# Linear attention and a gated FFN in one kernel: a new order of the first batch's loads and turns, the second batch's turns all by DMA, later loads for batches three and four

## The chip, the cores and the metric

The kernel runs on one core of one Trainium2 chip. The metric is the time of one execution on the device in microseconds (us). Before the change the median of 12 runs is 573.68 us (572.44 to 574.38). Engines are named as in the profile: PE (TensorE), DVE (VectorE), ACT (ScalarE), POOL (GpSimd) and SP (SyncE, which here only issues DMAs).

## The reference

For each of 8 batches and 8 heads, with 1024 tokens and a head dimension of 64:

```python
k_proj = einsum('ks,bhsd->bhkd', E, k)          # E: 64 x 1024
v_proj = einsum('ks,bhsd->bhkd', F, v)
scores = (q @ k_proj^T) / 8                     # 1024 x 64 per head
attn   = softmax(scores)
x      = (attn @ v_proj), heads side by side    # 8192 tokens x 512
g      = x @ w_gate                             # 512 x 1536
out    = (silu(g) * (x @ w_val)) @ w_out        # 8192 x 512, float32
```

Inputs are float32. The kernel works in bf16 with float32 sums; it leaves out the subtraction of the maximum and the 1e-09.

## The kernel before, in words

**The FFN sets the beat.** The 8192 tokens are cut into 16 chunks of 512 (two to a batch, `CH = 2`), and the 1536 hidden columns into 12 slices of 128. The main loop (L555) has 192 steps `t`, each one slice of one chunk: four matmuls of 128x512 for the gate (`f_g`, L331), four for the value (`f_v`, L337), and a part of the output projection of the chunk before (`f_y`, L350: four matmuls a piece). ACT takes the tanh of the gate, and DVE makes `(tanh + 1) * gate * value`, which is twice silu times value; the half is applied as the output row is copied out (L370).

**The attention is woven in by slots.** Step `t` has two slots: slot `2t` stands between gate and value, slot `2t+1` at the end of the step. `put(s, unit, ...)` books a unit of attention work or a load at slot `s`, and `place(b)` (L390) books all of batch `b`. The numbers are written out by hand. A slot fixes only where a unit stands in the order of each engine's instructions: a unit whose engine has nothing to wait for runs ahead of the slot's time. Loads booked at a slot stand ahead of the slot's other units (L545).

**The units.** `u_KV` projects k and v with E and F (eight matmuls each, L147). `u_KT` turns the projected k on PE and copies it into the block diagonal `BD`. q has to be turned to have its head dimension on the partitions: `u_T` does so with four PE transposes and a copy (L193), `u_TD` for a half batch with one DMA transpose on SP (L205). `u_S` makes the scores of four heads and 256 tokens (four matmuls, L227) and their exp on ACT; `u_R` sums and inverts on DVE; `u_N` multiplies, on POOL (L258), on DVE for two units of the first chunk. The attention matrix is turned as well: `u_A` with four PE transposes and a copy (L274), `u_AD` for a half batch with one DMA transpose on SP (L212). `u_PV` (L285) and, in the first chunk, `u_PV2` (L300) multiply it by the projected v and copy the result to `xT`, the FFN's input. `BY_DMA` (L31) lists the half batches that are turned by DMA: before, all from the second half of the second batch on.

**The loads.** k, v, q and the weights are float32 in memory and bf16 on the chip; the cast is made by the DMA, and such loads are issued by POOL, in the order of the program. So POOL's queue carries all of them in one row, and POOL's instruction order mixes loads with the normalizing of `u_N`. SP issues E and F, the DMA transposes and the output rows. `k` and `v` have two buffers each, `q` has four half batches.

**The head.** L427 to L521 are the first chunk, written out by hand. Nothing of the FFN can run before k, E, q, v, F and the first slices of the weights are there. `warm(n)` runs `n` matmuls on zeros on PE, whose results nobody reads. The first two steps are done for 256 tokens at a time.

Of the kernel before, what the change touches and what calls it, by code (L numbers as in the profile page):

```python
# [12 lines left out]
BF16 = mybir.dt.bfloat16  # L13
FP32 = mybir.dt.float32

B = 8
H = 8
# [10 lines left out]
CH = 2  # L28
CW = 512
NIT = B * CH * NFT  # L30
BY_DMA = [(b, ch) for b in range(1, B) for ch in range(CH)][1:]  # L31


@with_exitstack
def kernel(
# [47 lines left out]
    kb, vb, qb, xT, hT = {}, {}, {}, {}, {}  # L83

    def load_k(b, h0=0, h1=H):
        if h0 == 0:
            kb[b] = kv_pool.tile([P, H, NJ, D], BF16, name="kb", tag="kb")
        nc.gpsimd.dma_start(  # L88
            out=kb[b][:, h0:h1].rearrange("p h j d -> p h (j d)"),
            in_=k[b, h0:h1].rearrange("h (p j) d -> p h (j d)", j=NJ),  # L90
        )

    def load_v(b, heads=(0, H)):
        t = kv_pool.tile([P, H, NJ, D], BF16, name="vb", tag="vb")
        vb[b] = t
        for h0, h1 in zip(heads, heads[1:]):
            nc.gpsimd.dma_start(
                out=t[:, h0:h1].rearrange("p h j d -> p h (j d)"),
                in_=v[b, h0:h1].rearrange("h (p j) d -> p h (j d)", j=NJ),
            )  # L100

    def load_q(b, ch, parts=1):
        t = q_pool.tile([P, H, 4, D], BF16, name="qb", tag="qb")
        qb[b, ch] = t
        n = H // parts
        for i in range(parts):
            nc.gpsimd.dma_start(  # L107
                out=t[:, i * n : (i + 1) * n].rearrange("p h j d -> p h (j d)"),
                in_=q[b, i * n : (i + 1) * n].rearrange("h (p c j) d -> p c h (j d)", c=2, j=4)[:, ch],
            )  # L110

    def load_w_gv(c0, c1, which=(0, 1)):
        cs = slice(c0 * P, c1 * P)
        for wsrc, wdst in [((moe_w_gate, wg), (moe_w_val, wv))[i] for i in which]:
            nc.gpsimd.dma_start(
                out=wdst[:, :, cs],
                in_=wsrc[:, cs].rearrange("(t p) c -> p t c", p=P),
            )
# [11 lines left out]
    def bank(where, shape, dt, name):  # L130
        pool, tag = banks[where]
        return pool.tile(shape, dt, name=name, tag=tag)

    def copy(eng, out, in_):
        (nc.scalar.copy if eng is nc.scalar else eng.tensor_copy)(out=out, in_=in_)  # L135
# [51 lines left out]
    def u_T(b, u, at="a", eng=nc.scalar):  # L187
        ch, w = divmod(u, 4)
        g, i = divmod(w, 2)
        ps = bank(at, [P, 4, P], BF16, "qTp")  # L190
        src = qb[b, ch]
        for n in range(4):
            nc.tensor.transpose(  # L193
                out=ps[:, n, :],
                in_=src[:, 4 * g + n, 2 * i : 2 * i + 2, :].rearrange("p j d -> p (j d)"),
                identity=ident_bf[:],
            )
        t = aw.tile([P, 4, P], BF16, name="qT", tag="qT", bufs=4)
        copy(eng, t[:], ps[:])
        qT[b, u] = t  # L200
# [46 lines left out]
    def u_N(b, u):  # L247
        ch, w = divmod(u, 4)
        g, i = divmod(w, 2)
        if (b, ch) in BY_DMA:  # L250
            if (b, ch, "d") not in AA:
                AA[b, ch, "d"] = aw.tile([P, 4, H, KP], BF16, name="AAd", tag="AAd")
            a = AA[b, ch, "d"][:, 2 * i : 2 * i + 2, 4 * g : 4 * g + 4, :]
        else:
            a = AA[b, u] = aw.tile([P, 2, 4, KP], BF16, name="AA", tag="AA", bufs=4)
            a = a[:]
        eng = nc.vector if b == 0 and u in (2, 3) else nc.gpsimd
        eng.tensor_tensor(  # L258
            out=a.rearrange("p j h k -> p h j k"),
            in0=ee.pop((b, u))[:],  # L260
            in1=rr.pop((b, u))[:].unsqueeze(3).to_broadcast([P, 4, 2, KP]),
            op=ALU.mult,
        )
# [123 lines left out]
    def put(s, fn, *a):  # L387
        slots[s].append((fn, a))

    def place(b):  # L390
        s0 = 48 * (b - 1)
        if b == 1:
            put(30, u_TD, 1, 1)
            put(34, u_KV, 1, "k")
            put(36, u_KT, 1)
            put(40, u_KV, 1, "v")
            sa = (37, 38, 39, 40, 48, 50, 52, 54)
            tt = (35, 36, 37, 38)
            ta = (41, 42, 43, 44)
            put(57, u_AD, 1, 1)  # L400
            sp = (43, 44, 45, 46, 66, 67, 68, 69)
        else:
            put(s0, u_KV, b)
            put(s0 + 3, u_KT, b)
            o = 14 if b == 2 else 6
            put(s0 + (3 if b == 2 else -6), u_TD, b, 0)
            put(s0 + (5 if b == 2 else -4), u_TD, b, 1)
            sa = [s0 + o + 3 * j for j in range(NJ)]
            put(sa[3] + 4, u_AD, b, 0)
            put(sa[7] + 4, u_AD, b, 1)  # L410
            sp = [s0 + i for i in (39, 41, 43, 45, 57, 59, 61, 63)]
        for j in range(NJ):
            if (b, j // 4) not in BY_DMA:
                put(tt[j], u_T, b, j)
                put(ta[j], u_A, b, j)
            put(sa[j], u_S, b, j)
            put(sa[j] + 1, u_R, b, j)
            put(sa[j] + 1, u_N, b, j)
        for i in range(8):
            put(sp[i], u_PV, b, i // 4, i % 4)  # L420
# [3 lines left out]
            fn(*a)  # L424

    with tc.manual_schedule():
        load_k(0, 0, 4)  # L427
        ef = []
        for which, src in (("E", E), ("F", F)):
            raw = const.tile([KP, S], FP32, name=f"{which}raw")  # L430
            nc.sync.dma_start(out=raw[:], in_=src)
            ef.append(raw)
        zeros = const.tile([P, CW], BF16, name="zeros")
        nc.vector.memset(zeros[:], 0.0)
# [3 lines left out]
            nc.vector.memset(BD[i][:], 0.0)  # L438
            nc.vector.memset(BDV[i][:], 0.0)

        def turn(which):
            for half in range(2):
                ps = bank("v", [P, 4, KP], FP32, "efp")
                for i in range(4):
                    j = 4 * half + i
                    nc.tensor.transpose(
                        out=ps[:, i, :],
                        in_=ef[which][:, bass.ds(j, P, step=NJ)],
                        identity=ident_fp[:KP, :KP],
                    )  # L450
                js = slice(4 * half, 4 * half + 4)
                copy((nc.scalar, nc.vector)[which], (ET, FT)[which][:, js, :], ps[:])

        def warm(n):

            ps = bank("v", [P, CW], FP32, "warm")
            for _ in range(n):
                nc.tensor.matmul(
                    out=ps[:], lhsT=zeros[:, 0:P], rhs=zeros[:],
                    start=True, stop=True,  # L460
                )


        load_k(0, 4, 8)
        load_q(0, 0, 2)
        load_v(0, (0, 4, 8))
        load_w_gv(0, 1)
        load_w_gv(1, 2)
        load_w_gv(2, 4)
        warm(8)  # L470
        turn(0)
        turn(1)
        warm(7)
        u_KV(0, "k", (0, 4), at="y")
        warm(2)
        u_KT(0, at="v", prs=(0, 2))
        warm(2)
        u_KV(0, "k", (4, 8), at="y")
        warm(2)
        u_KT(0, at="v", prs=(2, 4))  # L480
        u_T(0, 0, "a", nc.scalar)
        u_T(0, 1, "a", nc.vector)
        u_T(0, 2, "a", nc.scalar)
        u_S(0, 0, "g")
        u_T(0, 3, "v", nc.vector)
        u_S(0, 2, "g")
        u_S(0, 1, "a")
        u_S(0, 3, "a")
        u_R(0, 0)
        u_N(0, 0)  # L490
        u_R(0, 2)
        u_N(0, 2)
        load_w_gv(4, 6, (0,))
        u_KV(0, "v", (0, 4), at="y")
        warm(1)
        u_A(0, 0, nc.scalar)
        u_R(0, 1)
        u_N(0, 1)
        u_R(0, 3)
        u_N(0, 3)  # L500
        u_A(0, 2, nc.scalar)
        u_KV(0, "v", (4, 8), at="y")
        load_w_gv(4, 6, (1,))
        load_q(0, 1)
        load_w_gv(6, 8)
        load_w_gv(8, 10)
        load_w_gv(10, 12)
        load_wo(0)
        load_wo(1)
        load_k(1)  # L510
        warm(1)
        u_PV2(0, 0, 0, 0, nc.scalar)
        u_PV2(0, 0, 1, 0, nc.vector)
        u_A(0, 1, nc.scalar)
        u_A(0, 3, nc.vector)
        f_mm(0, 0, 0, 0)
        f_mm(0, 0, 1, 0)
        u_PV2(0, 0, 0, 1, nc.scalar)
        u_PV2(0, 0, 1, 1, nc.vector)
        f_mm(0, 1, 0, 0)  # L520
        f_mm(0, 1, 1, 0)  # L521

# [7 lines left out]
        put(22, u_PV, 0, 1, 1)  # L530
        put(23, u_PV, 0, 1, 2)
        put(23, u_PV, 0, 1, 3)
        put(20, load_q, 1, 0)
        put(20, load_v, 1)
        put(20, load_q, 1, 1)
        for b in range(1, B):
            place(b)
        for b in range(2, B):
            s0 = 48 * (b - 1) - (12 if b == 2 else 24)
            put(s0, load_k, b)  # L540
            put(s0 + 2, load_v, b)
            put(s0 + 4, load_q, b, 0)
            put(s0 + 6, load_q, b, 1)

        for s in slots:  # L545
            slots[s].sort(key=lambda x: x[0] not in (load_k, load_v, load_q))
# [50 lines left out]
```

The softmax here doesn't subtract the row's maximum and nothing guards it: scores larger than these inputs give would overflow.

## Time and profile before

The profile shows one execution, which took 573.83 us on the device; the program's instructions span 572.1 us of it.

| What | Value |
|---|---|
| median of 12 runs | 573.68 us |
| profiled execution, its span | 573.83 us, 572.1 us |
| PE busy | 561.2 us (98%) |
| DVE, ACT, POOL busy | 336.8, 237.0, 107.9 us |
| chain that ended last | PE 94%, DMA 2%, POOL 1%, ACT 1% |
| moved by DMA | 61.34 MB, of it 29.89 MB by POOL's queue |
| DMA transposes | 13 of q, 13 of the attention matrix |

"Busy" is the time in which an engine has an instruction running. A view by engine names the instruction (by its line and the tiles it writes and reads, `out<-in`), how many there were, their mean duration, and what ended the idle time before them. The chain follows the last instruction back to what released it. A landing is the time from the issue of a DMA to the moment when its semaphore tells that all data are there. Loads that cast are counted in bytes as written, half of what is read.

### The profile page before, as it was taken

To read this page: it belongs to the slowest core of one execution; us is meant where nothing else is said; L and a number is where in the kernel's file an instruction comes from. 1 tells how busy PE (TensorE), PEld (TensorE's weight loads), DVE (VectorE), ACT (ScalarE), POOL (GpSimd) and SP (SyncE) were. 2 spreads that over 40 slices of the span, in tenths; PEclk is the share of its full clock that TensorE was granted. 3 is DMA by queue.
4 is the path that set the end of the run, shared out by engine and by line. 5 is a ranking of instruction groups with operands and counts; after the bars stand their busy time and mean duration, and the time that the engine had idled before them with its cause. 6 is when DMAs were issued, how large, how long until landed. Compare 5 with 4: busy or idle time off the path is not lost.

```text
span 572.1 us, 7867 instructions
## 1 busy us (share of the span) xinstructions
PE 561.2 (98%) x2910; PEld 268.5 (47%) x2967; DVE 336.8 (59%) x580; ACT 237.0 (41%) x416; POOL 107.9 (19%) x121
## 2 busy tenths in 40 slices
PE   8899999999999999999999999999999999999997
PEld 4654444444444444444444444444444444444444
DVE  2787566666466754766556665567546674554550
ACT  2665444354425434444335434354342543443232
POOL 6634121134002500124001330023200220000000
PEclk9999999999999999999999999999999999999999
DMA  9999993549901697038941499204990124100012
GB/s 160 195 200 206 202 160 75 92 68 181 215 34 45 114 189 152 18 75 129 195 100 38 63 173 195 66 20 92 192 178 36 45 49 74 38 37 26 30 39 92
DMA packets 105927, 61.34 MB, mean 107 GB/s; under 512 B 58016, under 2 KB 97696, under 8 KB 105888
## 3 DMA queue, kind: packets, MB, share of 16 engines
q0 software_dynamic: 42288, 29.89, 36.1%
q1 hardware_dynamic: 63312, 30.68, 25.3%
q8 instruction: 23, 0.38, 0.3%
q10 hardware_dynamic: 288, 0.26, 0.1%
q14 instruction: 16, 0.13, 0.1%
HBM read 60.29 MB, written 16.78 MB: 135 GB/s over the span
## 4 chain that ended last, share of the span: by engine, by line
PE 94%; DMA 2%; POOL 1%; ACT 1%; issue 1%; DVE 0%; POOLq 0%
PE yps L360 29%; PE vps L322 29%; PE gps L322 29%; PE kvp L147 3%; PE sc L227 2%; DMA vb<-in_v_dram 2%; PE pv L285 2%; PE aTp L274 0%; ACT xT L135 0%; PE qTp L193 0%; POOL kb L88 0%; PE kTp L172 0%; POOL qb L107 0%; ACT th L334 0%; PE pv L300 0%
## 5 line engine op out<-in xcount | busy, mean ns | idle before, releaser
L341 DVE SCALAR_TENSOR_TENSOR s<-th,gps 128x512 f32<-128x512 f32 x192 | 130.5, 680 | 138.0 <-ACT th L334 137.8
L322 PE MATMUL gps<-xT,wg 128*128 128x512 bf16 (+1 forms) x755 | 195.7, 377 | 1.2
L322 PE MATMUL vps<-xT,wv 128*128 128x512 bf16 (+1 forms) x761 | 195.9, 377 | 0.8
L360 PE MATMUL yps<-wo,hT 128*128 128x512 bf16 (+2 forms) x761 | 191.5, 376 | 0.8
L334 ACT ACTIVATE th<-gps 128x512 f32<-128x512 f32 x192 | 114.6, 597 | 162.6 <-PE gps L322 155.1
L346 DVE TENSOR_TENSOR hT<-s,vps 128x512 bf16<-128x512 f32 x192 | 132.0, 688 | 22.1 <-PE vps L322 1.5
L360 PEld LDWEIGHTS <-hT 128*128 128x128 bf16 x780 | 76.2, 98 | 89.9
L258 POOL TENSOR_TENSOR AAd<-ee,rr 128x512 bf16<-128x512 f32 x52 | 54.1, 1040 | 319.5 <-issue 168.5
L322 PEld LDWEIGHTS <-wv 128*128 128x128 bf16 x776 | 73.9, 98 | 82.9 <-issue 3.3
L322 PEld LDWEIGHTS <-wg 128*128 128x128 bf16 x776 | 74.0, 98 | 81.2 <-issue 0.6
L370 ACT ACTIVATE ysb<-yps 128x512 f32<-128x512 f32 (+1 forms) x65 | 38.4, 591 | 78.1 <-PE yps L360 74.4
L135 ACT CAST xT<-pv 128x512 bf16<-128x512 f32 x62 | 36.1, 585 | 51.3 <-PE pv L285 50.3
L242 DVE TENSOR_REDUCE zz<-ee 128x8 f32<-128x512 f32 x64 | 43.5, 679 | 17.9 <-ACT ee L231 17.9
L231 ACT ACTIVATE ee<-sc 128x512 f32<-128x512 f32 x64 | 37.9, 595 | 17.4 <-PE sc L227 17.4
L285 PE MATMUL pv<-AT,BDV 128*128 128x512 bf16 x60 | 22.6, 379 | 0.1
L227 PEld LDWEIGHTS <-qTd 128*128 128x128 bf16 x208 | 16.0, 98 | 12.3
L227 PE MATMUL sc<-BD,qTd 128*128 128x128 bf16 x208 | 20.1, 219 | 0.1
L135 DVE CAST BDV<-kvp 64x256 bf16<-64x256 f32 x14 | 6.0, 427 | 22.1 <-ACT ks L157 19.1
L258 POOL TENSOR_TENSOR AA<-ee,rr 128x512 bf16<-128x512 f32 x10 | 10.3, 1039 | 34.2 <-DVE rr L244 32.5
L244 DVE RECIPROCAL rr<-zz 128x8 f32<-128x8 f32 x64 | 13.0, 203 | 6.2
L147 PE MATMUL kvp<-vb,FT 128*64 128x512 bf16 (+1 forms) x72 | 15.5, 358 | 1.0 <-DMA vb<-in_v_dram 1.0
L147 PE MATMUL kvp<-kb,ET 128*64 128x512 bf16 (+1 forms) x72 | 15.5, 358 | 0.9 <-DMA kb<-in_k_dram 0.9
(49 smaller groups left out, 144.8 us busy)
## 6 DMA issues: line engine op xcount, KB each, us to landing
out_dram<-ysb SPq DMA_DIRECT2D x63, 256.0 KB, 2.3
qb<-in_q_dram POOLq DMA_DIRECT2D x15, 512.0 KB, 16.8
kb<-in_k_dram POOLq DMA_DIRECT2D x7, 1024.0 KB, 11.2
vb<-in_v_dram POOLq DMA_DIRECT2D x7, 1024.0 KB, 14.3
wo<-in_moe_w_out_dram POOLq DMA_DIRECT2D x2, 768.0 KB, 14.8
wg<-in_moe_w_gate_dram POOLq DMA_DIRECT2D x5, 256.0 KB, 11.4
wv<-in_moe_w_val_dram POOLq DMA_DIRECT2D x5, 256.0 KB, 11.4
kb<-in_k_dram POOLq DMA_DIRECT2D x2, 512.0 KB, 8.4
```

The costliest lines, as they stand in the source:

```text
L135: (nc.scalar.copy if eng is nc.scalar else eng.tensor_copy)(out=out, in_=in_)
L147: nc.tensor.matmul(out=t[lo : lo + 64, h0:h1].rearrange("p h d -> p (h d)"), lhsT=w[:, j, :], rhs=src[b][:, h0:h1, j, :], start=(j == 0), ...
L227: nc.tensor.matmul(out=ps[:, n, :], lhsT=t[:, n, :], rhs=BD[b % 2][:, 4 * g + n, :], start=True, stop=True)
L231: nc.scalar.activation(out=e[:].rearrange("p h j k -> p (h j k)"), in_=ps[:].rearrange("p a k -> p (a k)"), func=AF.Exp, scale=scale,)
L242: nc.vector.reduce_sum(out=z[:], in_=e[:], axis=AX.X)
L258: eng.tensor_tensor(out=a.rearrange("p j h k -> p h j k"), in0=ee.pop((b, u))[:], in1=rr.pop((b, u))[:].unsqueeze(3).to_broadcast([P, 4, 2 ...
L322: nc.tensor.matmul(out=ps[:, ts], lhsT=(wg, wv)[w][:, kt, f * P : (f + 1) * P], rhs=x[:, kt, ts], start=(kt == 0), stop=(kt == NKT - 1),)
L334: nc.scalar.activation(out=th[:], in_=ps[:], func=AF.Tanh, scale=0.5)
L341: nc.vector.scalar_tensor_tensor(out=s1[:], in0=th[:], scalar=1.0, in1=g[:], op0=ALU.add, op1=ALU.mult)
L346: nc.vector.tensor_tensor(out=hT[c][:, f, :], in0=s1[:], in1=ps[:], op=ALU.mult)
L360: nc.tensor.matmul(out=yy[c][:, cs], lhsT=hT[c][:, f, i * P : (i + 1) * P], rhs=wo[:, f, cs], start=(f == 0), stop=(f == NFT - 1),)
L370: nc.scalar.activation(out=ysb[:, cs], in_=yy[c][:, cs], func=AF.Copy, scale=0.5)
```

## The change

It has three parts.

**First batch.** The first four heads of k come as float32 through ACT's DMA queue, into two `kraw` tiles that share buffers with `qTd` and `AAd`, and are cast by copies on DVE and ACT. F moves from SP's to ACT's queue. `load_q` now cuts by token blocks instead of by heads: the first half (blocks 0 and 1) is issued ahead of k's second half, the other behind it. v comes in three pieces (four, two and two heads), each projected when it is there. F is turned in two halves, on either side of k's second projection. The score units, the attention turns and the `pv` units have a new order, three of four normalizings are on POOL, and the loads of the weights stand elsewhere among them. q's first half of batch two and its k are issued ahead of `wo`.

**Second batch.** `BY_DMA` takes in its first half, so eight PE turns (four of q, four of the attention matrix) become two DMA transposes; the units are booked anew.

**Later loads.** The loads of batch three move from slots 36, 38, 40 and 42 to 40, 40, 41 and 42, and its units by up to six slots; the loads of batch four move four slots later.

```diff
@@ -28,7 +28,7 @@
 CH = 2
 CW = 512
 NIT = B * CH * NFT
-BY_DMA = [(b, ch) for b in range(1, B) for ch in range(CH)][1:]
+BY_DMA = [(b, ch) for b in range(1, B) for ch in range(CH)]
 
 
 @with_exitstack
@@ -83,7 +83,7 @@
     kb, vb, qb, xT, hT = {}, {}, {}, {}, {}
 
     def load_k(b, h0=0, h1=H):
-        if h0 == 0:
+        if b:
             kb[b] = kv_pool.tile([P, H, NJ, D], BF16, name="kb", tag="kb")
         nc.gpsimd.dma_start(
             out=kb[b][:, h0:h1].rearrange("p h j d -> p h (j d)"),
@@ -91,23 +91,25 @@
         )
 
     def load_v(b, heads=(0, H)):
-        t = kv_pool.tile([P, H, NJ, D], BF16, name="vb", tag="vb")
-        vb[b] = t
+        if heads[0] == 0:
+            vb[b] = kv_pool.tile([P, H, NJ, D], BF16, name="vb", tag="vb")
+        t = vb[b]
         for h0, h1 in zip(heads, heads[1:]):
             nc.gpsimd.dma_start(
                 out=t[:, h0:h1].rearrange("p h j d -> p h (j d)"),
                 in_=v[b, h0:h1].rearrange("h (p j) d -> p h (j d)", j=NJ),
             )
 
-    def load_q(b, ch, parts=1):
-        t = q_pool.tile([P, H, 4, D], BF16, name="qb", tag="qb")
-        qb[b, ch] = t
-        n = H // parts
-        for i in range(parts):
-            nc.gpsimd.dma_start(
-                out=t[:, i * n : (i + 1) * n].rearrange("p h j d -> p h (j d)"),
-                in_=q[b, i * n : (i + 1) * n].rearrange("h (p c j) d -> p c h (j d)", c=2, j=4)[:, ch],
-            )
+    def load_q(b, ch, js=(0, 4)):
+        if js[0] == 0:
+            qb[b, ch] = q_pool.tile([P, H, 4, D], BF16, name="qb", tag="qb")
+        js = slice(*js)
+        nc.gpsimd.dma_start(
+            out=qb[b, ch][:, :, js, :].rearrange("p h j d -> p h (j d)"),
+            in_=q[b].rearrange("h (p c j) d -> p c h j d", c=2, j=4)[:, ch, :, js, :].rearrange(
+                "p h j d -> p h (j d)"
+            ),
+        )
 
     def load_w_gv(c0, c1, which=(0, 1)):
         cs = slice(c0 * P, c1 * P)
@@ -254,7 +256,7 @@
         else:
             a = AA[b, u] = aw.tile([P, 2, 4, KP], BF16, name="AA", tag="AA", bufs=4)
             a = a[:]
-        eng = nc.vector if b == 0 and u in (2, 3) else nc.gpsimd
+        eng = nc.vector if (b, u) == (0, 3) else nc.gpsimd
         eng.tensor_tensor(
             out=a.rearrange("p j h k -> p h j k"),
             in0=ee.pop((b, u))[:],
@@ -390,29 +392,26 @@
     def place(b):
         s0 = 48 * (b - 1)
         if b == 1:
+            put(22, u_TD, 1, 0)
+            put(29, u_KV, 1, "k")
+            put(32, u_KT, 1)
+            put(40, u_KV, 1, "v")
+            sa = (35, 36, 37, 38, 43, 44, 45, 47)
+            put(41, u_AD, 1, 0)
             put(30, u_TD, 1, 1)
-            put(34, u_KV, 1, "k")
-            put(36, u_KT, 1)
-            put(40, u_KV, 1, "v")
-            sa = (37, 38, 39, 40, 48, 50, 52, 54)
-            tt = (35, 36, 37, 38)
-            ta = (41, 42, 43, 44)
-            put(57, u_AD, 1, 1)
-            sp = (43, 44, 45, 46, 66, 67, 68, 69)
+            put(50, u_AD, 1, 1)
+            sp = (44, 45, 46, 46, 66, 67, 68, 69)
         else:
-            put(s0, u_KV, b)
-            put(s0 + 3, u_KT, b)
-            o = 14 if b == 2 else 6
-            put(s0 + (3 if b == 2 else -6), u_TD, b, 0)
-            put(s0 + (5 if b == 2 else -4), u_TD, b, 1)
+            put(s0 + (6 if b == 2 else 0), u_KV, b)
+            put(s0 + (9 if b == 2 else 3), u_KT, b)
+            o = 13 if b == 2 else 6
+            put(s0 + (7 if b == 2 else -6), u_TD, b, 0)
+            put(s0 + (9 if b == 2 else -4), u_TD, b, 1)
             sa = [s0 + o + 3 * j for j in range(NJ)]
             put(sa[3] + 4, u_AD, b, 0)
             put(sa[7] + 4, u_AD, b, 1)
             sp = [s0 + i for i in (39, 41, 43, 45, 57, 59, 61, 63)]
         for j in range(NJ):
-            if (b, j // 4) not in BY_DMA:
-                put(tt[j], u_T, b, j)
-                put(ta[j], u_A, b, j)
             put(sa[j], u_S, b, j)
             put(sa[j] + 1, u_R, b, j)
             put(sa[j] + 1, u_N, b, j)
@@ -424,11 +423,18 @@
             fn(*a)
 
     with tc.manual_schedule():
-        load_k(0, 0, 4)
+
+        kb[0] = kv_pool.tile([P, H, NJ, D], BF16, name="kb", tag="kb")
+        kraw = [aw.tile([P, 2, NJ * D], FP32, name="kraw", tag=tag) for tag in ("qTd", "AAd")]
+        for i in range(2):
+            nc.scalar.dma_start(
+                out=kraw[i][:],
+                in_=k[0, 2 * i : 2 * i + 2].rearrange("h (p j) d -> p h (j d)", j=NJ),
+            )
         ef = []
         for which, src in (("E", E), ("F", F)):
             raw = const.tile([KP, S], FP32, name=f"{which}raw")
-            nc.sync.dma_start(out=raw[:], in_=src)
+            (nc.sync if which == "E" else nc.scalar).dma_start(out=raw[:], in_=src)
             ef.append(raw)
         zeros = const.tile([P, CW], BF16, name="zeros")
         nc.vector.memset(zeros[:], 0.0)
@@ -438,9 +444,9 @@
             nc.vector.memset(BD[i][:], 0.0)
             nc.vector.memset(BDV[i][:], 0.0)
 
-        def turn(which):
-            for half in range(2):
-                ps = bank("v", [P, 4, KP], FP32, "efp")
+        def turn(which, at, halves=(0, 1)):
+            for half in halves:
+                ps = bank(at, [P, 4, KP], FP32, "efp")
                 for i in range(4):
                     j = 4 * half + i
                     nc.tensor.transpose(
@@ -449,7 +455,7 @@
                         identity=ident_fp[:KP, :KP],
                     )
                 js = slice(4 * half, 4 * half + 4)
-                copy((nc.scalar, nc.vector)[which], (ET, FT)[which][:, js, :], ps[:])
+                copy(nc.scalar, (ET, FT)[which][:, js, :], ps[:])
 
         def warm(n):
 
@@ -461,62 +467,71 @@
                 )
 
 
+        dve, act = nc.vector, nc.scalar
+        load_q(0, 0, (0, 2))
         load_k(0, 4, 8)
-        load_q(0, 0, 2)
-        load_v(0, (0, 4, 8))
+        load_q(0, 0, (2, 4))
+        load_v(0, (0, 4, 6, 8))
         load_w_gv(0, 1)
-        load_w_gv(1, 2)
-        load_w_gv(2, 4)
-        warm(8)
-        turn(0)
-        turn(1)
-        warm(7)
+        load_w_gv(1, 2, (0,))
+        warm(11)
+        turn(0, "v")
+        warm(4)
+        for h in range(4):
+            for n in range(2):
+                eng = act if (h, n) == (3, 1) else dve
+                ds = slice(256 * n, 256 * (n + 1)) if h == 3 else slice(0, 512)
+                if n == 0 or h == 3:
+                    copy(eng, kb[0][:, h].rearrange("p j d -> p (j d)")[:, ds], kraw[h // 2][:, h % 2, ds])
         u_KV(0, "k", (0, 4), at="y")
-        warm(2)
+        warm(1)
+        u_T(0, 0, "a", act)
         u_KT(0, at="v", prs=(0, 2))
-        warm(2)
-        u_KV(0, "k", (4, 8), at="y")
-        warm(2)
-        u_KT(0, at="v", prs=(2, 4))
-        u_T(0, 0, "a", nc.scalar)
-        u_T(0, 1, "a", nc.vector)
-        u_T(0, 2, "a", nc.scalar)
+        u_T(0, 2, "a", act)
+        turn(1, "a", (0,))
         u_S(0, 0, "g")
-        u_T(0, 3, "v", nc.vector)
-        u_S(0, 2, "g")
-        u_S(0, 1, "a")
-        u_S(0, 3, "a")
         u_R(0, 0)
         u_N(0, 0)
+        load_w_gv(1, 2, (1,))
+        warm(1)
+        u_KV(0, "k", (4, 8), at="y")
+        turn(1, "a", (1,))
+        u_KT(0, at="v", prs=(2, 4))
+        warm(1)
+        u_T(0, 1, "a", act)
+        u_A(0, 0, dve)
+        u_T(0, 3, "a", dve)
+        u_S(0, 2, "g")
         u_R(0, 2)
         u_N(0, 2)
-        load_w_gv(4, 6, (0,))
+        u_S(0, 1, "g")
+        u_R(0, 1)
+        u_N(0, 1)
+        load_w_gv(2, 4)
+        u_S(0, 3, "v")
+        u_R(0, 3)
+        u_N(0, 3)
         u_KV(0, "v", (0, 4), at="y")
         warm(1)
-        u_A(0, 0, nc.scalar)
-        u_R(0, 1)
-        u_N(0, 1)
-        u_R(0, 3)
-        u_N(0, 3)
-        u_A(0, 2, nc.scalar)
-        u_KV(0, "v", (4, 8), at="y")
-        load_w_gv(4, 6, (1,))
+        u_KV(0, "v", (4, 6), at="y")
+        u_PV2(0, 0, 0, 0, act)
+        u_A(0, 2, dve)
+        u_KV(0, "v", (6, 8), at="y")
+        u_A(0, 1, act)
+        u_PV2(0, 0, 1, 0, act)
+        u_A(0, 3, dve)
+        u_PV2(0, 0, 0, 1, dve)
+        load_w_gv(4, 6)
         load_q(0, 1)
-        load_w_gv(6, 8)
-        load_w_gv(8, 10)
-        load_w_gv(10, 12)
+        for f in (6, 8, 10):
+            load_w_gv(f, f + 2)
+        load_q(1, 0)
+        load_k(1)
         load_wo(0)
         load_wo(1)
-        load_k(1)
-        warm(1)
-        u_PV2(0, 0, 0, 0, nc.scalar)
-        u_PV2(0, 0, 1, 0, nc.vector)
-        u_A(0, 1, nc.scalar)
-        u_A(0, 3, nc.vector)
         f_mm(0, 0, 0, 0)
+        u_PV2(0, 0, 1, 1, act)
         f_mm(0, 0, 1, 0)
-        u_PV2(0, 0, 0, 1, nc.scalar)
-        u_PV2(0, 0, 1, 1, nc.vector)
         f_mm(0, 1, 0, 0)
         f_mm(0, 1, 1, 0)
 
@@ -530,17 +545,17 @@
         put(22, u_PV, 0, 1, 1)
         put(23, u_PV, 0, 1, 2)
         put(23, u_PV, 0, 1, 3)
-        put(20, load_q, 1, 0)
         put(20, load_v, 1)
         put(20, load_q, 1, 1)
         for b in range(1, B):
             place(b)
         for b in range(2, B):
-            s0 = 48 * (b - 1) - (12 if b == 2 else 24)
-            put(s0, load_k, b)
-            put(s0 + 2, load_v, b)
-            put(s0 + 4, load_q, b, 0)
-            put(s0 + 6, load_q, b, 1)
+            s0 = 48 * (b - 1) - (20 if b == 3 else 24)
+            at = (40, 40, 41, 42) if b == 2 else (s0, s0 + 2, s0 + 4, s0 + 6)
+            put(at[0], load_k, b)
+            put(at[1], load_v, b)
+            put(at[2], load_q, b, 0)
+            put(at[3], load_q, b, 1)
 
         for s in slots:
             slots[s].sort(key=lambda x: x[0] not in (load_k, load_v, load_q))
```

## The prediction

> **What bounds the kernel now.** I read the page's shares first, then PE's waits, then the chain of the head (the work ahead of the first gate matmul), then DMA stage by stage. The page:
>
> ```profile
> span 572.1 us, 7867 instructions
> PE 561.2 (98%) x2910; PEld 268.5 (47%) x2967; DVE 336.8 (59%) x580; ACT 237.0 (41%) x416; POOL 107.9 (19%) x121
> ...
> DMA  9999993549901697038941499204990124100012
> ```
>
> PE is the bound, and DMA is full in the first six slices (14.3 us each, to 86 us). PE's waits, longest total first:
>
> ```profile
> PE warm L458 <- DVE zeros L434: 1.2, 1, 1.2
> PE kvp L147 <- DMA vb<-in_v_dram: 1.0, 2, 0.6
> PE kvp L147 <- DMA kb<-in_k_dram: 0.9, 2, 0.7
> ```
>
> All seven rows of this view lie before 22 us; behind that it shows no wait of PE at all. So two things can shorten the run: less PE work behind 22 us, or an earlier start. The start's chain (start us, us, what) and DMA by stage:
>
> ```profile
> 6.19 13.47 DMA vb<-in_v_dram
> ...
> 22.37 0.56 PE gps L322 x4
> ```
>
> ```profile
> 2.00:4.00 2.00, 2.00 (x6) 0.76 (x5) 0.76 (x2) 0.02 (x1) 1.85 (x7) 1.00 0.98 225
> 4.00:9.00 5.00, 4.63 (x25) 2.70 (x24) 0.85 (x2) 0.75 (x2) 4.45 (x6) 1.00 1.06 156
> 9.00:17.00 8.00, 6.09 (x57) 4.09 (x58) 3.43 (x12) 3.27 (x7) 2.97 (x4) 1.00 1.31 202
> ```
>
> The last column is GB/s as written to SBUF. v's second half lands at 19.66, and 2.55 us later (22.21) the first gate matmul runs. The casting loads of POOL's queue reach 202 GB/s only after 9 us; until then the engines move less.
>
> [...] DMA in 67 to 71 us, a transpose beside loads, packets and MB:
>
> ```profile
> q0 software_dynamic: 612, 0.62, 91.4%
> q1 hardware_dynamic: 612, 0.16, 29.6%
> ```
>
> One packet each: 153 per us, and the loads fall from 202 to 155 GB/s.
>
> **The change, part by part.** Times in the clock of before.
>
> *Second batch.* Four groups of q turns (L193) and four of attention turns (L274) leave PE:
>
> ```profile
> 75.42 0.39 PE L274 MATMUL aTp<-ident_bf,AA 128*128 128x128 bf16 x4
> 75.65 1.03 PE L322 MATMUL gps<-xT,wg 128*128 128x512 bf16 x4
> 76.51 0.39 PE L274 MATMUL aTp<-ident_bf,AA 128*128 128x128 bf16 x4
> 76.73 1.03 PE L322 MATMUL vps<-xT,wv 128*128 128x512 bf16 x4
> ```
>
> A group holds PE from its start to the next start: 0.23 and 0.22 us. 8 x 0.22 = **1.76 us** of the bound. Their eight copies (0.59 on ACT, 0.42 on DVE) lie under matmuls: nothing. If no DMA is late, all of it is gain.
>
> *Slots as times.* Gate, v and y pieces take 0.86 each from start to start, so two slots are 1.72 and a y piece or two. Up to slot 28 nothing moves (v of step 14 at 52.14). Then k's projection (1.84 between the starts 58.28 and 60.12) runs at slot 29, 53.0, instead of 34, and with the turns gone and the scores at 35 to 38: score 0 at 62.8, score 3 at 67.0, v's projection at 70.6, first pv at 79.0.
>
> The two transposes by DMA cost PE nothing if they land in time:
>
> ```profile
> L205 SPq DMA_TRANSPOSE qTd<-qb x1: 7250/7250/7250, 62.8 to 62.8; - x1
> DMA to landing us min/median/max: 13.0/13.0/13.0
> ...
> L212 SPq DMA_TRANSPOSE AT<-AAd x1: 1763/1763/1763, 102.9 to 102.9; - x1
> DMA to landing us min/median/max: 4.3/4.3/4.3
> ```
>
> 4.3 us on idle engines, 13 among loads (15.6 at 200.6 us). *q's, first chunk:* q(1,0) now follows the weights (which end at 40.2) and lands about 42.9; the transpose, alone on SP's queue, lands by 60. Its score matmul (slot 35) comes at 62.8. The loads lose 50 of 205 GB/s for 13.5 us, 3.4 us of delay: with 1.5 MB now ahead of wo, its second half moves from 47.3 to about 58.3, needed at 61.1 (second y piece); k(1) about 48.2, needed at slot 29, 53.0; v(1) 64 against slot 40, 70.6; q(1,1) 66.5, its transpose 71, needed at 77.7. All covered, by 2 to 6 us. On SP the second transpose waits for q(1,1) with the first y store behind it (its data ready near 63.5, issued near 68.5 then; 70.08 in before, behind the same transpose): three ysb buffers, a third y row near 78, so nobody waits.
>
> *Attention, first chunk, is the tight one.* From score 3 (slot 38) to the first pv (slot 44) PE has gate, v and y pieces of 0.86 (x8 of y 1.73), v's projection 1.84 and turns of 0.22: 0.22+0.86+1.73+0.86+1.84+4x0.86+1.73+0.22+0.86+0.22 = 12.0 us. Score to normalized took 4.4 us (67.40 to 71.80), so the transpose must land within 7.5 us of its issue. The change puts k, v and q of batch three (slots 40 to 42) right behind that normalization on POOL, so they start together. The nearest precedent is a k load from idle with a store on SP 0.4 us behind it; GB/s in 40 slices of 259 to 266 us:
>
> ```profile
> GB/s 0 0 0 0 0 0 0 0 0 94 351 269 304 257 176 59 23 12 23 18 35 47 99 99 129 105 164 164 164 164 140 158 129 170 187 193 193 211 181 164
> ```
>
> k was issued at 259.46. The store runs first, from 260.6; k's packets are few until 263 and at 150 GB/s only near 264. So the transpose (2,069 packets at about 780 per us alone, 104.1 to 107.2) has 1.2 to 3.0 us nearly to itself (1,350), then shares: 300, 200, 200 per us. It ends near 5.4 and lands near 5.8, bounds 4.3 and 13. I take 5.8: no stall, margin 1.7 us. If k flowed at once, the stall would be 13.0 - 7.5 = 5.5 us.
>
> *Later loads.* k(2), v(2) come in by about 84 and 89, needed at slot 54, 93.6; the third batch's transposes start six slots ahead of their scores instead of eleven, 8 us against 4.3 to 5.3. Batch four's loads go from slot 72 to 76; they were ahead by 15 us (v landed 141.2, first used 156.6). Nothing.
>
> *The head.* Half of k as fp32 through ACT's queue, F behind it: 1.05 + 0.26 + 0.26 (E) = 1.57 MB from 2.0 us; POOL's part before v ends falls from 2.62 to 2.10 MB. Before: by 9 us POOL's queue had 0.71 MB, the other 1.91 at 202 take 9.45, so 18.45, and v landed 1.2 later. After: the 1.57 MB at 225 (E and F now) to 350 GB/s (the store's best); I take 300, 5.2 us, to 7.2; then 2.10 MB at 206 = 10.2, plus 0.7 since q comes in 256-byte pieces (the weights' are slower too: four of 128 KB took 4.0 us against 2.6), less 0.7 that POOL's queue moves meanwhile: 17.4, landed 18.6. Gain 1.05 us, bounds 0 and 1.8. Casting half of k is new on DVE: three of 128x512 and one half; near row FT's cast 128x256, 0.42 us; [...] I take 0.4: 1.4 us, done near 8.5, while k's half landed at 9.35 before. Covered by k's second half (11.9); if not, 1.4 us late. ACT's three issues (0.57 each, as SP's) end by 2.5, then its table load, 1.28: ready at 3.8, needed near 6. Were the load first ([...] here it stands at 0.74, ahead of nothing), k starts 1.3 us later and the head gains nothing.
>
> F lands near 8 behind k instead of at 5.7 and is first needed by v's projection, near 15.6: covered by 7 us less its turns (0.6 each half).
>
> After v: the last piece is two heads, eight matmuls half as wide, about 0.4 us less; but wg and wv of the first slice land 1.95 and 2.5 us behind v, and the load of wv for slot 12 (issued 23.51, landed 34.3, used 34.52) leaves PE 0.2 us. So only +0.15: head **1.2 us**. POOL now normalizes three score sets (1.04 each) ahead of the weights of slices 2 and 3: issue near 18 against 13.5, first needed by the engines about 20: covered by 0.5 us or so.
>
> Sum: 1.76 + 1.2 = 2.95 us. The profiled run took 573.83 for its span of 572.1, and is 0.15 over the median: span 569.15, time 573.68 - 2.95 = **570.7**.
>
> **Rivals.** *Head gives nothing* (E's 225 GB/s for k, or the weights behind POOL's normalizing late): 573.68 - 1.76 = 571.9. For it: every byte that v waits for still passes the same engines. Against: they were under-used until 9 us. *Attention's transpose late*: full sharing from the start, stall 5.5: 570.7 + 5.5 = 576.2, slower. It decides from a landing 7.5 us after issue; slower by over 0.2% (1.15 us, about what can be told from no change here) needs 11.6. For it: every transpose that met loads in flow took 9.4 to 18.2 us. Against: this one is issued as the loads start. *Half of that stall*, 2 to 4 us: 573.7, no difference. *The q transpose or wo late* would be 1 to 3 us in the same place, 60 to 65 us.
>
> **Chances.** Forecast 0.48 (569.8 to 571.5), head nothing 0.15, half stall (with wo or q late) 0.14, full stall 0.18, a slower head 0.05. Faster 0.62, same 0.14, slower 0.24: a few of the first two cases fall short. The range 569.6 to 575.6 leaves out less than 1 in 20 below and the upper part of the full stall.
>
> **What would show it.** L193 and L274 gone behind 50 us; v landing near 18.6 and the first gps near 21; PE's waits naming no AT; in the trace the first AT issue landing in under 7 us near 77. A pv wait on AT of over 3 us, or a gate matmul waiting on wv near 33, makes it wrong.

## The result, and the profile after

The changed kernel takes 580.49 us (median; 579.49 to 581.04) against 573.62 us before: ratio 1.0119, with a 95% interval of 1.0110 to 1.0128. It is slower by 6.9 us, where the forecast was 570.7 us and the range ended at 575.6. The profiled execution took 579.54 us, 5.7 more than that of before (573.83); it lies 0.95 us under its median, while the one of before lay 0.2 us over its own, so about 1.2 of the 6.9 us can't be placed in the trace.

In 40 slices of the span (a slice is 14.4 us here), the busy tenths of PE and the clock granted to it, first before the change:

```profile
PE   8899999999999999999999999999999999999997
...
PEclk9999999999999999999999999999999999999999
```

Then in the changed kernel, with its span:

```profile
span 577.8 us, 7823 instructions
...
PE   8999969999999999999999999999999999999997
...
PEclk9999989999999999999999999999999999999999
```

Only the sixth slice of the changed kernel (72 to 87 us) stands out: PE is at 6 and its clock at 8, where both were 9. One place holds the loss. PE's waits there (engine, line, what it waited for: us in total, times, longest):

```profile
PE pv L287 <- DMA AT<-AAd: 5.7, 1, 5.7
PE warm L464 <- DVE zeros L440: 1.2, 1, 1.2
PE kvp L149 <- ACT BDV L137: 0.6, 1, 0.6
```

The waits for v and k, 1.0 and 0.9 us before, are nearly gone; at their place stands one wait of 5.7 us. The chain of the changed kernel around it (start us, us, what; `AAd` is the normalized attention matrix, `AT` the turned one, `pv` its product with v):

```profile
70.39 1.05 POOL AAd L260
71.44 0.02 issue
71.46 13.13 DMA AT<-AAd
84.59 0.05 issue
84.64 0.61 PE pv L287
85.25 1.71 PE vps L324 x4
```

The last normalizing of batch two's first chunk ends at 71.43, the DMA transpose of its attention matrix is issued at 71.46 and lands 13.1 us later; the pv matmul that reads it starts at 84.64. Before the wait PE had run to 78.99. The four value matmuls behind it take 1.71 us in place of 0.86.

To see where the time goes I compare the start of the tanh of a step (it follows the step's gate matmuls) with that of the kernel before. Step 2 is the first full one, step 7 lies behind the last step that waits for weights, steps 14 and 32 lie ahead of and behind all that moved in batch two.

| Kernel | step 2 | step 7 | step 14 | step 32 | step 191 |
|---|---|---|---|---|---|
| changed kernel | -1.58 | -0.61 | -0.47 | +5.46 | +5.46 |

Early is negative, in us. From step 32 on nothing changes any more, so all of it is a gain of 0.47 in the head and a loss of 5.93 between steps 14 and 32: -1.8 for the turns off PE, +5.8 for the wait (78.86 to 84.64), +1.9 for the slow pieces behind it. The other 0.25 us of the span lies behind the last tanh, and no run here says why.

### The profile page after: what moved, and what is told of

Read it like the earlier page. It is cut to its first block, busy times and chain, and to the rows that moved or that the text cites. A ratio compares the mean times of both kernels' runs of the same rounds, so it can differ in the third digit from the quotient of the medians.

```text
span 577.8 us, 7823 instructions
## 1 busy us (share of the span) xinstructions
PE 561.7 (97%) x2883; PEld 267.3 (46%) x2939; DVE 335.4 (58%) x577; ACT 236.6 (41%) x417; POOL 109.1 (19%) x122
## 4 chain that ended last, share of the span: by engine, by line
PE 90%; DMA 4%; DVE 2%; POOL 1%; ACT 1%; issue 1%; DVEq 0%; POOLq 0%
PE yps L362 28%; PE vps L324 27%; PE gps L324 26%; PE kvp L149 2%; DMA AT<-AAd 2%; PE sc L229 2%; PE pv L287 2%; DMA wv<-in_moe_w_val_dram 2%; PE warm L464 1%; DVE zz L244 1%; POOL AA L260 0%; POOL wg L117 0%; DVE hT L348 0%; PE qTp L195 0%; ACT xT L137 0%
## 5 line engine op out<-in xcount | busy, mean ns | idle before, releaser
L260 POOL TENSOR_TENSOR AAd<-ee,rr 128x512 bf16<-128x512 f32 x56 | 58.2, 1040 | 351.1 <-issue 157.2
L324 PEld LDWEIGHTS <-wv 128*128 128x128 bf16 x776 | 74.1, 98 | 84.6 <-issue 4.1
L324 PEld LDWEIGHTS <-wg 128*128 128x128 bf16 x776 | 73.9, 98 | 82.2 <-DMA wg<-in_moe_w_gate_dram 1.0
L229 PEld LDWEIGHTS <-qTd 128*128 128x128 bf16 x224 | 17.3, 98 | 13.5 <-issue 0.6
L229 PE MATMUL sc<-BD,qTd 128*128 128x128 bf16 x224 | 21.7, 219 | 0.1
L149 PE MATMUL kvp<-vb,FT 128*64 128x512 bf16 (+2 forms) x80 | 15.6, 338 | 0.8 <-ACT BDV L137 0.6
L107 POOL DMA_DIRECT2D qb<-in_q_dram x17 | 15.5, 914 | 0.6 <-DMA wv<-in_moe_w_val_dram 0.6
```

Of the source, the lines that this page charges most:

```text
L149: nc.tensor.matmul(out=t[lo : lo + 64, h0:h1].rearrange("p h d -> p (h d)"), lhsT=w[:, j, :], rhs=src[b][:, h0:h1, j, :], start=(j == 0), ...
L229: nc.tensor.matmul(out=ps[:, n, :], lhsT=t[:, n, :], rhs=BD[b % 2][:, 4 * g + n, :], start=True, stop=True)
L260: eng.tensor_tensor(out=a.rearrange("p j h k -> p h j k"), in0=ee.pop((b, u))[:], in1=rr.pop((b, u))[:].unsqueeze(3).to_broadcast([P, 4, 2 ...
L324: nc.tensor.matmul(out=ps[:, ts], lhsT=(wg, wv)[w][:, kt, f * P : (f + 1) * P], rhs=x[:, kt, ts], start=(kt == 0), stop=(kt == NKT - 1),)
```

## The experiments

**Is it the loads that start beside the transpose?** My theory after the result: batch three's loads, issued by POOL in the same moment (71.38), take the DMA engines' turns. The rival: the transpose is late anyway, by the output row that SP issued ahead of it, or by the q transpose before that. The edit holds the loads until the transpose has landed: a copy of two elements on POOL reads its result ahead of them.

```diff
+        touch = const.tile([P, 2], BF16, name="touch")
+        put(42, lambda: nc.gpsimd.tensor_copy(out=touch[:], in_=AT[1, 0][:, 0, 0, 0:2]))
...
-            at = (40, 40, 41, 42) if b == 2 else (s0, s0 + 2, s0 + 4, s0 + 6)
+            at = (43, 43, 43, 43) if b == 2 else (s0, s0 + 2, s0 + 4, s0 + 6)
```

> The changed kernel, with batch three's k, v and q loads issued only when the first attention transpose of batch two has landed (a two-element copy on POOL reads its result ahead of them). Own theory, the loads that start beside it slow it: it lands 4.3 to 5 us after its issue instead of 13.1, the pv wait of 5.7 us on AT and the 1.9 us of slow clock behind it are gone, so 580.5 - 7.6 = 572.9 us (571.5 to 574, the loads start 4 us later and could be late for k's projection at slot 54). Rival, it is slow by itself or by the output row stored just ahead of it on SP: it lands after 10 us or more again, the wait stays over 3 us and the time over 577.

Measured: 571.6 us, ratio to before 0.9961 (0.9947 to 0.9976). The attention transpose in that trace:

```profile
L214 SPq DMA_TRANSPOSE AT<-AAd x1: 1923/1923/1923, 71.3 to 71.3; - x1
DMA to landing us min/median/max: 4.3/4.3/4.3
```

Its issue is the same, the output row stands ahead of it as before, and it lands in 4.3 us. No wait for it is left, and no later wait has come in its place: batch three's k and v land at 86.6 and 92.3 us, in time. Issued 4.5 us later than in the changed kernel (75.84 against 71.38), k even lands 1.3 us earlier than there (87.9) and v 0.6 us (92.9). The rival falls. This kernel is also 2 us faster than the one before the change.

**Is the slow stretch behind the wait PE's clock?** In the changed kernel (us; busy us of PE, PEld, DVE, ACT, POOL with instructions; PE's clock; DMA share; GB/s):

```profile
80.00:81.00 1.00, 0.00 (x0) 0.00 (x0) 0.38 (x1) 0.00 (x0) 1.00 (x1) 1.00 1.23 164
81.00:82.00 1.00, 0.00 (x0) 0.00 (x0) 0.00 (x0) 0.00 (x0) 0.00 (x0) 0.84 1.25 185
82.00:83.00 1.00, 0.00 (x0) 0.00 (x0) 0.00 (x0) 0.00 (x0) 0.00 (x0) 0.50 1.20 225
88.00:88.50 0.50, 0.50 (x3) 0.20 (x2) 0.40 (x2) 0.00 (x0) 0.00 (x0) 0.50 1.36 218
88.50:89.00 0.50, 0.50 (x7) 0.38 (x6) 0.08 (x1) 0.03 (x1) 0.28 (x1) 1.00 1.31 197
```

The clock falls to half while PE is idle (from 81.7 us) and comes back only at 88.5, 3.9 us after PE has work again. The edit gives PE something to do in the wait:

```diff
+        if b == 1:
+            put(44, warm, 26, "a")
         for i in range(8):
             put(sp[i], u_PV, b, i // 4, i % 4)
...
```

> The changed kernel, with 26 matmuls on zeros (26 x 0.215 = 5.6 us) on PE ahead of the first pv of batch two, where PE waits 5.7 us for AT. Nothing useful is added or removed. If PE's half clock behind the wait (granted 0.50 from 84.6 to 88 us) comes of its idling, the clock stays 1.00 and the pieces behind the wait take 0.86 us again: 580.5 - 1.9 = 578.6 us. If the slow pieces have another cause (loads in flight, the DMA's own demand): no change, 580.5 us.

Measured: 578.36 us, ratio to before 1.0076 (1.0061 to 1.0091). The same loads are in flight, at the same rate, but the clock stays whole:

```profile
84.60:86.00 1.40, 1.40 (x7) 0.60 (x7) 0.20 (x1) 0.59 (x1) 0.00 (x0) 1.00 1.22 214
86.00:88.00 2.00, 2.00 (x14) 1.03 (x13) 1.71 (x4) 1.06 (x3) 0.47 (x1) 1.00 1.27 205
```

So of the 6.9 us about 2 are the price of having waited, on top of the wait itself: 2.1 by the medians, and 1.7 by the steps of the last table (+4.23 between steps 14 and 32 here, against +5.93), which leave out that the head of this profiled run was 0.3 us earlier.

**The two halves of the change, each alone.** First the head on the kernel before: `BY_DMA`, `place` and all loads from batch two on are those of before.

> Only the first batch's part of the change on the kernel before: the new loads and order of the head; batch two's turns and all later loads as before, k of batch two behind wo again. The trace of the changed kernel says a gain of 0.5 us (step 14's v starts at 51.67 against 52.14): 573.1 us. My forecast's term was 1.2 us: 572.4. Rival, the head gives nothing: 573.6.

Measured: 573.0 us, ratio 0.9989 (0.9982 to 0.9996): a gain of 0.6 us (0.2 to 1.0); in its profiled run step 14 is 0.95 us early, against 0.47 in the changed kernel. A single trace doesn't give the head's gain to better than some tenths: the eight profiled kernels with this head and its order of loads are 0.39 to 0.95 us early at step 14 (last table). Then the rest on the kernel before, with the head of before.

> Only the rest of the change on the kernel before: batch two's first chunk turned by DMA, its q and k ahead of wo, the later loads; the head as before. Own theory: 573.6 - 1.76 (eight turns off PE) + 5.7 (pv wait on AT) + 1.9 (slow clock) = 579.4 us, 1.010 of before. If the head's new order were what makes the transpose late, the wait would be under 2 us here and the time near 572.

Measured: 579.38 us, ratio 1.0097 (1.0079 to 1.0116). Its attention transpose lands after 12.1 us, and pv waits 4.6 us for it. The loss between steps 14 and 32 is there without the new head (4.46 us, against 5.93).

**Where the head's gain went.** In the changed kernel steps 2 to 5 are 1.58 us early, step 7 only 0.61: step 6's gate matmuls wait from 31.9 to 32.56 for weights that land at 32.5. POOL issues the weights of slices 2 and 3 behind two normalizings, at 18.97 and 19.77 us. The edit, on the kernel with the loads held, only moves their issue ahead of the normalizings:

```diff
         load_w_gv(1, 2, (1,))
+        load_w_gv(2, 4)
         warm(1)
...
-        load_w_gv(2, 4)
         u_S(0, 3, "v")
```

> The first kernel of these experiments (loads held until AT has landed), and on POOL the weights of slices 2 and 3 issued ahead of the two normalizings that stood before them (17.0 to 19.0 us in the changed kernel). Own theory of the lost head gain: POOL's queue ran dry behind the first weights because those issues came at 19.0 and 19.8 us; the gate matmuls of step 2 to 5 are 1.4 to 1.6 us early, but step 6 waits for its weights and keeps 0.9 to 1.0. With the issues earlier the weights of step 6 land 0.7 us sooner: 571.6 - 0.6 = 571.0 us, step 6 at least 1.4 us early. Rival, the engines are full there anyway, so the order of issue moves nothing: 571.6 us, step 6 early by 1.0.

Measured: 571.1 us, ratio to before 0.9957 (0.9944 to 0.9971). Step 7 is 1.49 us early, step 14 1.36. What the DMA engines did from 20 to 22 us, in the changed kernel and then with the weights issued first:

```profile
20.00:22.00 2.00, 1.83 (x18) 1.49 (x19) 1.02 (x2) 1.14 (x3) 2.00 (x4) 1.00 1.36 129
```

```profile
20.00:22.00 2.00, 1.79 (x17) 1.46 (x18) 1.00 (x3) 1.17 (x3) 2.00 (x3) 1.00 1.61 187
```

129 GB/s against 187: the queue had run dry for want of issued loads. The step table shows it more sharply than the times do, whose intervals overlap with those of the first experiment: between steps 2 and 7 the eight kernels with the old order lose 0.54 to 0.97 us, and this one loses nothing.

**Does a start from idle slow the transpose, or the loads' being there?** Batch three's k and v are issued at slot 21, so that they are in flow when the attention transpose comes.

```diff
-            at = (40, 40, 41, 42) if b == 2 else (s0, s0 + 2, s0 + 4, s0 + 6)
+            at = (21, 21, 43, 43) if b == 2 else (s0, s0 + 2, s0 + 4, s0 + 6)
```

> The changed kernel, with batch three's k and v issued right behind q of batch two (slot 21 instead of 40), so that they are in flow when the attention transpose is issued near 71.5 us; its q behind the normalizing as before. Own theory, a transpose and loads take turns packet by packet: k and v need 10 us from 66 us on, stretched by batch two's second q transpose, to about 78 or 79 us; so the attention transpose moves at 150 packets per us until then, about 900 of 2069, and then alone: it lands at 80 to 82 us, wait 1 to 3 us, time 573 to 576. If what slows it is the slow start of the loads from idle, not their being there: it lands within 6 us and the time is near 572.

Measured: 584.3 us (two executions only, 583.38 and 585.23), ratio 1.0188 (1.0168 to 1.0207), worse than either theory said. PE's waits:

```profile
PE sc L229 <- DMA qTd<-qb: 5.3, 1, 5.3
PE pv L287 <- DMA AT<-AAd: 4.4, 1, 4.4
```

I had left out batch two's second q transpose, which meets the same loads: it lands after 15.6 us instead of 4.3, and holds SP from 67.1 to 73.9, with two output rows behind it. So the attention transpose is issued only at 75.4 and takes 14.4 us, with batch three's q behind k and v at once. That a transpose suffers by loads in flow is confirmed twice (15.6 and 14.4 us); the sizes of my expectation were wrong by one transpose and the queue behind it. Whether loads that start from idle slow it more than loads in flow, this run can't say, since two transposes and three kinds of loads met in it.

**How much lead is enough?** One or two multiplies of 128x512 on POOL, whose results nobody reads, stand between the last normalizing and batch three's loads, which stay at slots 40 to 42. The diff is that of one; the other kernel has `range(2)`.

```diff
+        hold = const.tile([P, 2, CW], BF16, name="hold")
+
+        def held():
+            nc.gpsimd.tensor_tensor(
+                out=hold[:, 0], in0=zeros[:], in1=zeros[:], op=ALU.mult
+            )
+
+        for i in range(1):
+            put(39.5, held)
...
             run_slot(2 * t + 1)
+            run_slot(2 * t + 1.5)
```

> The changed kernel, with one more 128x512 multiply on POOL (0.5 to 1 us, result unused) between the last normalizing of batch two's first chunk and batch three's loads. In the changed kernel 1,035 of 2,069 transpose packets were through when the loads' packets began, 2.6 us after their issue. Own theory: each us of lead is worth 700 packets alone, or 6 us of the shared stretch; with 1 us, 1,700 are through and the transpose lands near 78 us, the wait is under 1 us, and the time 572 to 575. Rival, lead does not matter, the transpose is slow beside loads at any point: 580.

> As the run with one more multiply on POOL, but with two (1 to 2 us of lead). Own theory: all packets are through when the loads begin, it lands within 5 us of its issue, no wait on AT, 571.5 to 572.5 us. Rival, as there: 580.

Measured: with one 571.99 us, ratio 0.9984 (0.9974 to 0.9994), from 571.33 to 575.06 us; with two 571.52 us, ratio 0.9967 (0.9953 to 0.9981), from 571.31 to 572.04. With one, the loads are issued 0.9 us behind the transpose, which then lands after 9.4 us; with two, 2.0 us behind, and it lands after 5.0. Two are enough. With one it stands on the edge: in the profiled run (573.77 us) pv waits 1.9 us; by their times, down to 571.33, others hardly wait. (The expectation's 1,035 packets of the changed kernel is the count at 74.5 us; when the loads' first packets began, at 74.1, it was 761.) And the profiled run with one shows something that the counts of data packets don't explain. By 75.7 us, when the loads' first packets begin, 2,024 of the transpose's 2,048 data packets are through, and the last are at 76.2; yet it lands at 80.7. DMA of that kernel from 76.3 to 80.8 us, by queue (packets, MB, share):

```profile
q0 software_dynamic: 626, 0.64, 106.8%
q1 hardware_dynamic: 32, 0.00, 1.0%
```

The 32 are packets of 4 bytes, as the transposes counted here have them at their end. In the run with the loads held the transpose's queue moves nothing behind 75.1 us, and it lands at 75.6. Here it lands 4.5 us behind its last data (76.2 to 80.7), while POOL's loads run. What keeps it back, no run shows.

**Only q turned by DMA.** The attention turns of the chunk go back to PE, the loads stay as in the change.

```diff
+AT_BY_DMA = BY_DMA[1:]
...
-        if (b, ch) in BY_DMA:
+        if (b, ch) in AT_BY_DMA:
...
-            put(41, u_AD, 1, 0)
+            for j, at in enumerate((40, 41, 42, 43)):
+                put(at, u_A, 1, j)
```

> The changed kernel, with the attention turns of battwo's first chunk back on PE (four groups of four, slots 40 to 43); q of that chunk stays turned by DMA, and batch three's loads stay at slots 40 to 42. Own theory, only the attention transpose stood in the loads' way: no wait on a transpose, four of eight turns gained, 573.6 - 0.6 (head) - 0.9 = 572.1 us. Rival, batch three's loads at these slots hurt in themselves (k or v late at slot 54, or other waits): over 574 us.

Measured: 572.14 us, ratio 0.9975 (0.9967 to 0.9982). The loads' slots do no harm in themselves (this kernel has no wait on AT, and none on k or v of batch three); what they harm is the transpose (13.1 us in the changed kernel, 4.3 with the loads held).

**The turns off PE, alone.** The rest of the change on the kernel before, with the loads held as in the first experiment.

> The kernel before with batch two's and the later part of the change (head as before), and batch three's loads held until the attention transpose of batch two's first chunk has landed. What is left is the eight turns off PE: 573.6 - 1.76 = 571.8 us. If holding the loads also costs something later (k, v or q of batch three late), less of it: 572 to 573.

Measured: 572.26 us, ratio 0.9983 (0.9975 to 0.9992). The steps of all these kernels, early or late in us, each from one profiled execution. The last kernel has the head of before and still reads +0.21 at step 2, so a few tenths between two rows of the first three columns mean nothing.

| Kernel | step 2 | step 7 | step 14 | step 32 |
|---|---|---|---|---|
| loads behind AT | -1.44 | -0.79 | -0.64 | -2.42 |
| warm matmuls in the wait | -1.73 | -0.92 | -0.79 | +3.44 |
| head only | -1.84 | -1.09 | -0.95 | -0.95 |
| rest only | -0.05 | -0.05 | -0.05 | +4.41 |
| weights first, loads behind AT | -1.49 | -1.49 | -1.36 | -3.15 |
| loads in flow | -1.69 | -0.85 | -0.71 | +11.15 |
| attention on PE | -1.42 | -0.54 | -0.39 | -1.29 |
| held by one | -1.48 | -0.72 | -0.58 | -0.31 |
| held by two | -1.38 | -0.84 | -0.70 | -2.49 |
| rest, loads held | +0.21 | +0.21 | +0.21 | -1.58 |

Between steps 14 and 32 the kernels without a wait gain 1.78 or 1.79 us (loads behind AT, weights first, held by two, rest with loads held), and the one with half of the turns 0.90.

## Why the prediction was wrong, point by point

**The turns off PE: right.** 1.76 us forecast, 1.79 measured wherever no transpose is late.

**The attention transpose: the step that failed.** I let it land 5.8 us after its issue, within the 7.5 us that PE leaves; it took 13.1. The 7.5 were right: issued at 71.46, first pv due at 78.9. So was the start of its packets, 1.2 us after the issue. Three things in between were not. First, how much it moves ahead of the loads. DMA of the changed kernel from 72.4 to 74.1 us, when the loads' first packets come (2.7 us after k's issue), the transpose's queue:

```profile
q1 hardware_dynamic: 761, 0.19, 68.4%
```

At 74.46, where the forecast's lead of 3.0 us ends, it had moved 1,007 packets in place of 1,350. It starts slowly, before any packet of the loads; its issue on SP took 2.7 us, against 1.9 with the loads held. No run separates why. Second, the sharing. From 75 to 82 us:

```profile
q0 software_dynamic: 730, 0.74, 81.1%
q1 hardware_dynamic: 841, 0.22, 49.3%
```

That is 120 of its packets per us against about 104 of the loads, where I had 300 and then 200. I had quoted one for one, 153 per us, for loads in flow, and then assumed that loads starting from idle would leave the transpose the rest; in fact they left it less than the 153. Third, the completion: its last data packet ended at 82.75 and it landed at 84.59, 1.8 us later (0.5 with the loads held). Of the 7.3 us by which it came late, 5.9 lie in the first two (last packet 11.3 us after the issue, where I had 5.4) and 1.4 in the third.

My precedent was to blame: an output row of 256 KB in 128 packets that was all but through when the first packet of the k load beside it came (its last began at 261.9, k's first at 261.7). This transpose of 512 KB has 2,048 packets of 256 bytes, and they need about 2.6 us alone (72.5 to 75.1 with the loads held). The fitting precedents, 9.4 to 18.2 us, I had listed as the rival's evidence and set aside.

**The rival came true, and was priced too low.** "Attention's transpose late" stood at 0.18 with a stall of 5.5 us and 576.2 us in all. The stall was 5.7. The time was 4.3 us higher. In the trace, PE's half clock behind the wait, in no term of mine, makes 1.9 us of it; the head gave 0.5 us there, not 1.2, which makes 0.7; the wait makes 0.3 (78.86 to 84.64 is 5.8) and the end of the span 0.2. The other 1.1, but for rounding, are the medians' distances from the profiled executions. A pv wait of over 3 us, which I had named as a sign of being wrong, is what the trace shows. My range ended at 575.6, below this rival's own 576.2. The point from which the rival decides, a landing after 7.5 us, held wherever PE came to that place undelayed: landings after 4.3 and 5.0 us gave no wait, 9.4 us one of 1.9, 12.1 us one of 4.6, 13.1 us one of 5.7.

**The head: the mechanism right, one term wrong.** v landed at 18.53 (18.6 forecast), and the first gate matmul ran at 20.96 (near 21 forecast); k's half was cast by 8.3 (8.5 forecast), though DVE's three casts of 128x512 took 0.79, 0.41 and 0.43 us where I had 0.4 each, my estimate, which no trace had shown. That ACT's issues would run ahead of its table load I had assumed too; it held: they start at 0.74, the table load at 2.33. The failed term is the cover of "0.5 us or so" for the weights behind POOL's normalizing: they were issued at 18.97 and 19.77, not near 18, there was no cover, and of 1.4 to 1.8 us at step 2 the dry queue took 0.5 to 1.0.

**The covers in batch two held.** q's first transpose landed at 61.3, 19.1 us after its issue, against 62.6, when its score matmul ran: I had 60 against 62.8, so this cover was thinner than said. `wo`'s second half came at 57.8 (58.3 forecast) and v at 63.4 (64).

## What to carry to other kernels

The DMA transposes here had 2,048 packets of 256 bytes each and got about one packet for each one of the loads beside them (612 to 612 in the kernel before, 841 to 730 in the changed one), so that of batch two's first attention matrix took 4.3 us or 13.1 by what was issued within the next two microseconds. Put the large loads behind it in their issuing engine's order, by a dependence if need be, and not only behind it in a table of slots. When an early start is bought by reordering issues on an engine that also computes, check that its queue never runs dry. And price a stall of PE like those of 4.6 and 5.7 us here with the slow clock that came with them, 1.6 to 2 us.

## What I had not expected of the hardware

- Two stalls of PE cost more than their length. In the changed kernel the clock fell to 0.50 after 2.7 us of idling and came back 3.9 us after work did, and about 2 us of time were the price (580.49 against 578.36 with matmuls on zeros in the wait). With the rest of the change alone pv waits 4.6 us and the granted clock is 0.997 in the mean of the span (0.993 in the changed kernel, 1.000 before); its loss of 4.46 us between steps 14 and 32 is some 1.6 us more than the wait less the 1.79 gained there. The profiled run with a wait of 1.9 us had a mean clock of 1.000.
- The end of a transpose trailed its data: held by one, it landed 4.5 us behind its last data packet, when loads from idle began just then; with the loads held it was 0.5 us.
- Loads issued earlier landed later: beside the transpose k took 16.5 us from issue to landing, and 10.7 when issued behind it, so that 4.5 us of earlier issue gained nothing.
- A transpose moved 120 packets per us beside loads that had started from idle, and 153 beside loads in flow. These are two stretches of two kernels; no run isolates the start from idle as the cause.
